# A fused attention, expert and gated-product kernel: unit stores moved earlier, three low-part subtractions per expert change given to GpSimd, and the first gather reordered

## The chip, the cores and the metric

The kernel runs on one core of a Trainium2 chip. The metric is device time in microseconds (us) of one execution. The engines are called as the profile calls them: PE (TensorE, the matmuls), DVE (VectorE), ACT (ScalarE), POOL (GpSimd) and SP (SyncE, which here only issues DMAs).

## What is computed

Three parts follow each other, on 4 x 448 = 1792 tokens of 768 numbers:

```python
scores = q @ k.T / sqrt(64) - log(448)
x = sigmoid(scores) @ v                       # 4 batches, 12 heads of 64
e = argmax(cosine(x, expert_emb) / tau)       # one of 8 experts for each token
y = gate_w * (relu(x @ w1[e]) @ w2[e])        # w1 768x1024, w2 1024x768
out = ((y @ w_a) * (y @ w_b)) @ w_out         # 768x1536, 768x1536, 1536x768
```

## The kernel before, in words

**Arithmetic in two parts.** A product in float32 is made of three cheaper ones: every operand is split into a high part, rounded by a copy, and a low part, the operand minus the high part. `split` (line 786) does it for weights: ACT copies the raw tile to the high part (line 787), and an engine, `nc.vector` unless told otherwise, subtracts (line 788). PE multiplies high by high, high by low and low by high.

**Attention** (`attention`, line 492) is a loop over 24 pairs of heads, numbers 0 to 23, with one more turn to drain. A turn transposes q and k of the next pair (`tr_pair`, line 554), loads q, k and v of later pairs (`load`), computes scores and sigmoids in two halves (matmul line 579, ACT line 584), multiplies by v (line 601), and turns the outcome to tokens (`x_tok`, lines 616 and 617). Between these steps `pump` advances generators that hold the routing of a finished batch (`route`) and the tables of a half of the tokens (`tables`): which tokens stand in which block of 128, and which expert a block has. Once the flags of the first half stand, `first_expert` returns seven small steps, an empty one and six that split one slice of `w1` of the first expert each and load the slice after the next (lines 917 to 931). One is taken per turn from `early_w`, and what is left runs after the loop. When the tables stand, `gather(0)` (line 812, an indirect DMA issued by POOL) fetches the tokens of the first block.

**Background units.** The weights of the third part are rounded ahead of time in 144 units, of which 48 run in the first two parts. `prep_tick` (line 231) does four things for successive units: it stores finished ones (`prep_store`, line 226, a DMA on SP's queue), finishes one (`prep_finish`, DVE line 216, two operands in SBUF), loads one (`prep_load`, SP) and begins one (`prep_unit`: DVE lines 199 and 201, ACT lines 203 and 205, POOL line 206). The tile `ab`, which ACT writes at line 205, has three buffers, so a unit waits until the store of the unit three before has read its own. In attention most turns have one tick at their end, the turns 9, 15 and 21 two.

**Experts.** `block1` (line 990) handles one block of 128 tokens: first matmul `p1` (line 891, or 911 to 913 for the first block), turning of the hidden layer and its split (ACT 969 and 970, DVE 973, tile `hTl`), and second matmul `p2` (line 1012). All weights of an expert lie in SBUF as high and low parts, `w1h`/`w1l` in six slices of 1024 columns and `w2h`/`w2l` in eight of 768. Where the next block has another expert, the flag `chg` is 1 and its 14 slices are split inside the block and the next one, in this order on ACT and DVE: `w1` slices 0 and 1, the tokens of the next block (`x_load`, DVE line 841), `w1` slices 2 to 5, a tick, the block's output `y` (DVE 1082), `prep_finish`, `w2` slices 0 to 3; in the next block `w2` slices 4 and 5 after its first `p1` and 6 and 7 in its second. The raw weights of the expert after that are loaded by SP in the block that uses the earlier ones: `load_new(1)` at its beginning, `load_new(2)` after its first tick, each into tiles that the splits must have left. POOL has, in order, the gather for the block after the next, the additions of the ticks and the scatter of `y` (line 1104). Each engine works its queue in program order.

**The third part** (`glu`) streams the rounded weights and is not touched.

The change moves three lines of `attention`, a `prep_store()` of `block1`, and adds an engine argument in `split_w` (line 801).

Of the kernel before, what the change touches and what calls it, by code (L numbers as in the profile page):

```python
# [9 lines left out]
F32 = mybir.dt.float32  # L10
# [14 lines left out]
def build(ctx: ExitStack, tc: tile.TileContext, q, k, v, emb, tau, w1, w2, wa, wb, wo, out, dbg=None, stop=None):  # L25
# [6 lines left out]
    nc = tc.nc  # L32
# [193 lines left out]
    def prep_store(dma=nc.sync):  # L226
        while prep_out:
            o, t = prep_out.pop(0)
            dma.dma_start(out=o, in_=t)
# [248 lines left out]
    def pump(ps=(True, LATE, END)):  # L478

        while bg:  # L480
            job = next((j for j in bg if j[2]), bg[0])
            if job[1] and job[1] not in ps:
                return
            job[2] = False
            try:
                job[1] = next(job[0])
                return
            except StopIteration:
                bg.remove(job)


    def attention():
# [21 lines left out]
        def load(i, names):  # L514
            if i >= NPR:
                return
            b, hp = pairs[i]
            for nm in names:
                src = dict(q=q, k=k, v=v)[nm]
                sv = src[b, 2 * hp:2 * hp + 2].rearrange("h (p c) d -> p h c d", c=NCH)  # L520
                if nm == "v":
                    t = raw_p.tile([P, 2, NCH, D], F32, tag=nm, name=nm, bufs=4)
                    nc.sync.dma_start(out=t[:, :, :NCH - 1, :], in_=src[b, 2 * hp:2 * hp + 2, :KC].rearrange(
                        "h (p c) d -> p h (c d)", c=NCH - 1))
                    nc.sync.dma_start(out=t[half_of(i), :, NCH - 1, :],
                                      in_=src[b, 2 * hp:2 * hp + 2, KC:].rearrange("h p d -> p h d"))
                elif nm == "k":
                    t = raw_p.tile([P, NCH, 2, D], F32, tag=nm, name=nm, bufs=3)
                    dma = nc.scalar if i < 2 else nc.sync
                    for j in range(2):  # L530
                        dma.dma_start(out=t[:, :NCH - 1, j, :], in_=src[b, 2 * hp + j, :KC].rearrange(
                            "(p c) d -> p c d", c=NCH - 1))
                    nc.sync.dma_start(out=t[half_of(i), NCH - 1], in_=src[b, 2 * hp:2 * hp + 2, KC:].rearrange(
                        "h p d -> p h d"))
                else:
                    t = raw_p.tile([CP, NCH, 2, D], F32, tag=nm, name=nm, bufs=3)
                    for j in range(2):
                        nc.sync.dma_start(out=t[:, :, j, :], in_=sv[:, j])
                raw[i, nm] = t

        def tr_pair(i):

            if i == 1:
                pt = [p() for p in av_ps]
                parts = [(pt[s][:, :S], slice(s, s + 1)) for s in range(2)]
            else:
                both = ps_t.tile([P, 2, 512], F32, tag="pt", name="pt")
                pt = [both[:, s] for s in range(2)]
                parts = [(both[:, :, :S], slice(0, 2))]
            for s, nm in enumerate(("q", "k")):  # L550
                t = raw.pop((i, nm))
                for c in range(NCH):
                    cs, r = (slice(c * CP, (c + 1) * CP), slice(0, CP)) if nm == "q" else key_chunk(i, c)
                    nc.tensor.transpose(out=pt[s][:, cs], in_=t[r, c].rearrange("p h d -> p (h d)"), identity=ident[r, r])
            hi = qk_p.tile([P, 2, S], F32R, tag="qkh", name="qkh")
            lo = qk_p.tile([P, 2, S], F32R, tag="qkl", name="qkl")
            for src, ss in parts:
                h, l = (t[:, ss, :] if src.ndim == 3 else t[:, ss.start, :] for t in (hi, lo))
                nc.scalar.copy(out=h, in_=src)
                nc.vector.tensor_tensor(out=l, in0=src, in1=h.bitcast(F32), op=ALU.subtract)  # L560
            QK[i] = (hi, lo)
# [83 lines left out]
        for i in range(NPR + 1):  # L645
            if 0 < i and i + 1 < NPR:
                tr_pair(i + 1)
            load(i + 3, "qk")
            load(i + 2, "v")
            if i < NPR:  # L650
                score_half(i, 0)
            misc["ps"] = av_ps[i % 2]
            if i == NPR:
                one, turn = misc["ps"], [0]

                def either():
                    turn[0] ^= 1
                    return ps_s.tile([P, 2, 512], F32, tag="ps", name="pm2")[:, 0] if turn[0] else one()

                misc["ps"] = either  # L660
            pump((True,))
            if early_w is None and misc.get("flags0"):
                early_w = first_expert()
            if misc.get("tables0") and not misc.get("gathered"):
                gather(0)
                misc["gathered"] = True
            if early_w:
                early_w.pop(0)()
            if 1 <= i <= NPR:
                av_part(i - 1, 0)  # L670
            pump((True,))
            if i < NPR:
                score_half(i, 1)
            pump((LATE,))
            if i % 2 and i >= 2:
                x_tok(i - 2)
            if 1 <= i <= NPR:
                av_part(i - 1, 1)
            if i == NPR:
                both = ps_s.tile([P, 2, 512], F32, tag="ps", name="px0")  # L680
                x_load(0, [both[:, hf] for hf in range(2)])
                gather(1)
            if i >= 2:
                if i % 2 == 0:
                    x_tok(i - 2)
                b, hp = pairs[i - 2]
                if hp == NP - 1:
                    routed(b)
            if i < 3:
                prep_load(i)  # L690
            elif i < NPR:
                prep_tick(nc.sync)
                if i % 6 == 3 and i > 3:
                    prep_tick(nc.sync, 1)
            pump((END,))

        while early_w:
            early_w.pop(0)()
# [87 lines left out]
    def split(hi, lo, src, f32_hi, eng=nc.vector):  # L786
        nc.scalar.copy(out=hi, in_=src)  # L787
        eng.tensor_tensor(out=lo, in0=src, in1=f32_hi, op=ALU.subtract)  # L788
# [8 lines left out]
    def load_w(which, expert, pair):  # L797
        t, src = (r1[pair], w1) if which == 1 else (r2[0][:, 2 * pair:2 * pair + 2, :], w2)
        nc.sync.dma_start(out=t, in_=src[expert, 2 * pair * P:2 * (pair + 1) * P, :].rearrange("(k p) c -> p k c", p=P))

    def split_w(which, kk, pool=None):
        hi, lo = (w1h, w1l) if which == 1 else (w2_t["h"], w2_t["l"])
        t = r1[kk // 2][:, kk % 2, :] if which == 1 else r2[0][:, kk, :]
        split(hi[kk], lo[kk], t, hi[kk].bitcast(F32))

    def gather(b):
        if b >= NBLK:
            return
        ph = 0 if b < LIVE0 else 1
        t = xg_t[b % len(xg_t)]  # L810
        j = b - TB[ph][0]
        nc.gpsimd.indirect_dma_start(out=t, out_offset=None, in_=xs_d[:CAP[0], :] if ph == 0 else xs_d[:, :],
                                     in_offset=bass.IndirectOffsetOnAxis(ap=idx[ph][:, j:j + 1], axis=0))
        xg[b] = t
# [166 lines left out]
    def moe(r2_p):  # L981
# [8 lines left out]
        def block1(b, chg, was_new, load, e_load, live):  # L990
            def when_new(fn, chg=chg):
                if chg is not None:
                    with tc.If(chg == 1):  # L993
                        fn()

            def load_new(which):
                for i in range((KD if which == 1 else KF) // 2):
                    load_w(which, e_load, i)
# [5 lines left out]
            def p1(hf, inner):  # L1004
                p1_half(b, hf, ps_1.tile([P, FH], F32, tag="p1", name="p1"),
                        mx_p.tile([P, FH], F32, tag="h", name="h"), inner)
# [31 lines left out]

            if b > 0:
                when_new(lambda: load_new(1), load)  # L1040
                p1(0, lambda: None)
                when_new(lambda: split_new(2, KF // 2, KF - 2), was_new)
                tick()

                def rest():
                    when_new(lambda: split_new(2, KF - 2, KF), was_new)

                p1(1, rest)
                tick()
                if b < LIVE - 1:  # L1050
                    prep_tick()
                when_new(lambda: load_new(2), load)
# [37 lines left out]
                    nc.vector.scalar_tensor_tensor(out=yo[:PH], in0=yp[hf][PH:, :HD], scalar=gt[:PH], in1=yo[:PH],  # L1090
                                                   op0=ALU.mult, op1=ALU.add)

            if 0 < b < LIVE - 1:
                prep_store()
            either(b, y_whole, y_half)
            if live is not None:
                tc.mark_branch_hint_location(f"live{b + 1}", live, [ET.Activation, ET.DVE])
# [8 lines left out]

        for i in range(2, KF // 2):
            load_w(2, e_of[0], i)

        def block(b, was_new=None):  # L1110
            nx = b + 1
# [253 lines left out]
```

## Time and profile before

| what | us |
|---|---|
| median of 3 runs (lowest, highest) | 1075.32 (1074.67, 1077.29) |
| the profiled execution, its own time | 1076.83 |
| its span, first to last instruction | 1074.9 |

In the profiled execution the first turns of attention begin near 14 us, attention ends near 210 us, the blocks of tokens run to about 538 us, and the third part to the end. The profile says for each engine how long it was busy, which instruction ended each idle stretch, and what clock was granted to PE. An instruction that had to wait after it was begun shows a longer time, not an idle stretch. A row of the timeline merges equal instructions that follow each other (x4), and its time runs from the first's start to the last's end.

### The profile page before, as it was taken

The page shows a single profiled execution, that of the slowest core. Times are in us where ns is not written, and L with a number is a line of the kernel's source. Part 1 is how long each engine was busy: PE and PEld are TensorE (multiplying, and loading weights), DVE is VectorE, ACT ScalarE, POOL GpSimd, SP SyncE. Part 2 cuts the span into 40 slices and gives each one's busy share as a digit, 9 for nine tenths or more (in the row PEclk, how much of TensorE's full clock was granted, in tenths as well). Part 3 has the DMA queues.
Part 4 walks back from the last instruction along what each step waited for, and adds up shares of the span by engine and source line. Part 5 has one row for each costly group of instructions (what it writes and reads, how often), then busy time and mean ns, then how long its engine had stood idle before and what let it go on. Part 6 is the DMA issues. An engine that isn't in the chain of part 4 may idle for free. (4 is left out here: it accounts for less than half of the span.)

```text
span 1074.9 us, 17443 instructions
## 1 busy us (share of the span) xinstructions
PE 1049.5 (98%) x5916; PEld 848.5 (79%) x5916; DVE 592.3 (55%) x1061; ACT 510.4 (47%) x803; POOL 154.2 (14%) x222
## 2 busy tenths in 40 slices
PE   7999999999999999999999999999999999999998
PEld 4554555488878977998978888888888888888997
DVE  2566698868793869372256786333333333333553
ACT  5777676543673777262155554333323322332542
POOL 2031221423222222221102222000000000000000
PEclk9999999999999999999999999999999999999999
DMA  6687769648589778822184644292220272210820
GB/s 161 170 207 200 186 175 260 197 146 292 174 307 331 253 262 305 317 86 101 47 279 176 221 132 145 105 361 109 88 88 1 107 289 89 89 45 1 350 105 30
DMA packets 118051, 187.84 MB, mean 175 GB/s; under 512 B 53928, under 2 KB 89000, under 8 KB 113072
## 3 DMA queue, kind: packets, MB, share of 16 engines
q1 hardware_dynamic: 113296, 171.10, 47.5%
q0 software_dynamic: 3040, 14.94, 3.9%
q8 instruction: 56, 0.92, 0.3%
q10 hardware_dynamic: 1600, 0.39, 0.2%
q14 instruction: 59, 0.48, 0.1%
HBM read 154.17 MB, written 32.24 MB: 173 GB/s over the span
## 5 line engine op out<-in xcount | busy, mean ns | idle before, releaser
L1229 PE MATMUL ab<-yh,whi 128*128 128x512 f32 (+1 forms) x576 | 209.3, 363 | 0.4 <-DVE yl L788 0.4
L1230 PE MATMUL ab<-yl,whi 128*128 128x512 f32 (+1 forms) x576 | 209.3, 363 | 0.2 <-DVE yl L788 0.2
L1231 PE MATMUL ab<-yh,wlo 128*128 128x512 f32 (+1 forms) x576 | 209.0, 363 | 0.0
L206 POOL TENSOR_TENSOR m<-m,raw 128x384 int32<-128x384 int32 x72 | 75.9, 1054 | 353.8 <-DVE m L201 193.4
L1231 PEld LDWEIGHTS ab<-yh,wlo 128*128 128x128 f32 x576 | 108.8, 189 | 17.3 <-DVE wlo L788 0.3
L1229 PEld LDWEIGHTS ab<-yh,whi 128*128 128x128 f32 x576 | 108.8, 189 | 16.3 <-ACT whi L787 0.5
L1230 PEld LDWEIGHTS ab<-yl,whi 128*128 128x128 f32 x576 | 108.8, 189 | 16.2 <-DVE yl L788 0.9
L1262 PE MATMUL o<-whi,gh 128*128 128x512 f32 x336 | 114.7, 341 | 0.0
L1263 PE MATMUL o<-whi,gl 128*128 128x512 f32 x336 | 113.7, 338 | 0.0
L1264 PE MATMUL o<-wlo,gh 128*128 128x512 f32 x336 | 113.0, 336 | 0.0
L1237 DVE TENSOR_TENSOR m<-ab,a 128x512 f32<-128x512 f32 (+1 forms) x48 | 30.0, 624 | 144.6 <-issue 126.5
L787 ACT CAST gh<-m 128x512 fp32r<-128x512 f32 (+1 forms) x48 | 27.2, 567 | 166.4 <-DVE m L1237 166.4
L584 ACT ACTIVATE a<-ps,bias_s 128x896 f32<-128x896 f32 x96 | 92.9, 1006 | 26.5 <-PE ps L579 25.8
L788 DVE TENSOR_TENSOR wlo<-r,whi 128x768 fp32r<-128x768 f32 x76 | 68.6, 954 | 57.3 <-ACT whi L787 57.3
L787 ACT CAST whi<-r 128x768 fp32r<-128x768 f32 x76 | 58.9, 833 | 54.6 <-PE o L1263 46.0
L601 PE MATMUL av<-a,v 128*64 128x448 f32 (+1 forms) x384 | 79.8, 571 | 2.0 <-DVE xtok L617 2.0
L788 DVE TENSOR_TENSOR wlo<-wx,whi 128x768 fp32r<-128x768 f32 x57 | 51.2, 954 | 44.0 <-ACT whi L787 44.0
L1262 PEld LDWEIGHTS o<-whi,gh 128*128 128x128 f32 x336 | 63.4, 189 | 8.2
L1263 PEld LDWEIGHTS o<-whi,gl 128*128 128x128 f32 x336 | 63.4, 189 | 7.5
L1264 PEld LDWEIGHTS o<-wlo,gh 128*128 128x128 f32 x336 | 63.1, 188 | 7.4
L973 DVE SCALAR_TENSOR_TENSOR hTl<-px,hTh 128x512 fp32r<-128x512 f32 x35 | 24.1, 689 | 73.2 <-ACTq L993 63.7
L787 ACT CAST whi<-wx 128x768 fp32r<-128x768 f32 x57 | 43.8, 832 | 40.7 <-PE o L1263 36.0
(271 smaller groups left out, 1847.6 us busy)
## 6 DMA issues: line engine op xcount, KB each, us to landing
r<-in_moe_w_dram SPq DMA_DIRECT2D x28, 768.0 KB, 14.6
wx<-wm SPq DMA_DIRECT2D x18, 1152.0 KB
r<-wm SPq DMA_DIRECT2D x17, 1152.0 KB, 5.6
r<-in_moe_w_dram SPq DMA_DIRECT2D x18, 1024.0 KB, 10.9
raw<-in_moe_w_a_dram SPq DMA_DIRECT2D x24, 384.0 KB, 3.7
raw<-in_moe_w_b_dram SPq DMA_DIRECT2D x24, 384.0 KB, 3.7
raw<-in_moe_w_out_dram SPq DMA_DIRECT2D x24, 384.0 KB, 3.9
wm<-ab SPq DMA_DIRECT2D x48, 192.0 KB, 2.6
```

The lines of the kernel that those rows point to most:

```text
L206: nc.gpsimd.tensor_tensor(out=m, in0=m, in1=low, op=ALU.add)
L584: nc.scalar.activation(out=a[r], in_=ps[:n, :, :S], func=AF.Sigmoid, bias=bias_s[:n], scale=qscale)
L601: nc.tensor.matmul(av[w][j * D:(j + 1) * D, :S], lhsT=raw[w, "v"][r, j, c, :], rhs=a[r, j, :], start=first, stop=last)
L787: nc.scalar.copy(out=hi, in_=src)
L788: eng.tensor_tensor(out=lo, in0=src, in1=f32_hi, op=ALU.subtract)
L1229: nc.tensor.matmul(ps[:, :n], lhsT=hi[:, s, cs], rhs=yh[:, kk, :n], start=kk == 0, stop=False)
L1230: nc.tensor.matmul(ps[:, :n], lhsT=hi[:, s, cs], rhs=yl[:, kk, :n], start=False, stop=False)
L1231: nc.tensor.matmul(ps[:, :n], lhsT=lo[:, s, cs], rhs=yh[:, kk, :n], start=False, stop=kk == KD - 1)
L1237: nc.vector.tensor_tensor(out=m, in0=ps[:, :n], in1=a, op=ALU.mult)
L1262: nc.tensor.matmul(t[:, d0:d1], lhsT=gh[:, cs], rhs=hi[:, 2, d0:d1], start=first, stop=False)
L1263: nc.tensor.matmul(t[:, d0:d1], lhsT=gl[:, cs], rhs=hi[:, 2, d0:d1], start=False, stop=False)
L1264: nc.tensor.matmul(t[:, d0:d1], lhsT=gh[:, cs], rhs=lo[:, 2, d0:d1], start=False, stop=last)
```

## The change

In attention, finished units are stored at the beginning of a turn, ahead of its loads; the step of `early_w` is taken before the turn's first `pump`, where it was taken after it (so the first, empty one is taken a turn later); and `gather(0)` goes out at the end of the turn in which the tables are done, where it went out in the next turn after the first `pump`. In `block1` the store of finished units goes from the end of the block to the beginning of the next, behind `load_new(1)`. From the first block on, GpSimd does the subtraction of slice 3 of `w1` and of slices 2 and 5 of `w2`.

```diff
@@ attention, in a turn
             if 0 < i and i + 1 < NPR:
                 tr_pair(i + 1)
+            prep_store()
             load(i + 3, "qk")
             load(i + 2, "v")
...
+            if early_w:
+                early_w.pop(0)()
             pump((True,))
             if early_w is None and misc.get("flags0"):
                 early_w = first_expert()
-            if misc.get("tables0") and not misc.get("gathered"):
-                gather(0)
-                misc["gathered"] = True
-            if early_w:
-                early_w.pop(0)()
...
             pump((END,))
+            if misc.get("tables0") and not misc.get("gathered"):
+                gather(0)
+                misc["gathered"] = True
@@ split_w
+    on_pool = {}
+
     def split_w(which, kk, pool=None):
...
-        split(hi[kk], lo[kk], t, hi[kk].bitcast(F32))
+        split(hi[kk], lo[kk], t, hi[kk].bitcast(F32), nc.gpsimd if kk in on_pool.get(which, ()) else nc.vector)
@@ block1
             if b > 0:
                 when_new(lambda: load_new(1), load)
+                if b < LIVE:
+                    prep_store()
                 p1(0, lambda: None)
...
-            if 0 < b < LIVE - 1:
-                prep_store()
             either(b, y_whole, y_half)
@@ moe, before block(0)
+        on_pool.update({1: (3,), 2: (2, 5)})
```

## Rows read from the trace of the kernel before

**Rows 1.** The page, busy time of each engine (share of the span) and instructions.

```profile
PE 1049.5 (98%) x5916; PEld 848.5 (79%) x5916; DVE 592.3 (55%) x1061; ACT 510.4 (47%) x803; POOL 154.2 (14%) x222
```

**Rows 2.** Waits of PE, whole run: us in total, times, longest.

```profile
PE ps L579 <- ACT a L584: 1.6, 1, 1.6
...
PE p L1012 <- ACT hTh L970: 1.5, 2, 0.7
...
PE px L962 <- ACT h L914: 1.3, 3, 0.8
```

**Rows 3.** Stretches: length, busy us of the engines, granted clock, DMA share, GB/s.

```profile
106.00:109.00 3.00, 3.00 (x13) 1.28 (x10) 0.62 (x1) 2.35 (x4) 0.00 (x0) 0.50 0.68 195
...
284.00:305.00 21.00, 21.00 (x115) 19.00 (x114) 20.68 (x28) 17.82 (x28) 5.71 (x5) 1.00 0.69 248
...
460.00:480.00 20.00, 19.96 (x111) 18.04 (x110) 17.19 (x20) 15.56 (x24) 5.01 (x2) 1.00 0.14 46
```

**Rows 4.** Timeline of attention, turns 10 to 12, DVE, SP and ACT: start, us, what.

```profile
92.48 1.02 DVE L216 SCALAR_TENSOR_TENSOR ab<-ab,m 128x384 f32<-128x384 f32 x2
...
99.59 1.01 SPq L229 DMA_DIRECT2D wm<-ab  x2
...
102.19 0.56 ACT L205 ACTIVATE ab<-raw 128x384 f32<-128x384 bf16 x1 [3.91 <-DMA wm<-ab]
```

**Rows 5.** Timeline behind the end of attention: DVE and PE.

```profile
212.90 0.69 DVE L617 COPY xtok<-pm 112x512 f32<-112x512 f32 x1
...
214.64 0.39 PE L912 MATMUL p<-w1l,xh 128*128 128x512 f32 x1
```

**Rows 6.** Timeline, POOL and DVE at three places.

```profile
300.55 1.02 POOL L206 TENSOR_TENSOR m<-m,raw 128x384 int32<-128x384 int32 x1 [6.91 <-DVE m L201]
...
300.82 2.97 DVE L788 TENSOR_TENSOR w1l<-r,w1h 128x1024 fp32r<-128x1024 f32 x2
...
303.71 1.01 DVE L841 TENSOR_TENSOR xl<-px,xh 128x384 fp32r<-128x384 f32 x2
...
388.08 2.36 DVE L788 TENSOR_TENSOR w1l<-r,w1h 128x1024 fp32r<-128x1024 f32 x2 [0.25 <-ACT w1h L787]
...
205.35 2.06 POOL L206 TENSOR_TENSOR m<-m,raw 128x384 int32<-128x384 int32 x1 [5.65 <-ACT w1h L787]
...
206.46 0.98 DVE L311 TENSOR_SCALAR om<-sg 112x32 f32<-112x32 f32 x1
```

**Rows 7.** Groups of POOL instructions by shape: busy us, mean ns.

```profile
L377 POOL TENSOR_TENSOR py<-oh_all,beg 112x64 f32<-112x64 f32 x2 | 0.6, 322 | 0.2
```

**Rows 8.** Timeline at the sixth change of expert: DVE and POOL.

```profile
471.85 5.36 DVE L788 TENSOR_TENSOR w2l<-r,w2h 128x768 fp32r<-128x768 f32 x6
...
472.70 3.56 POOL L1104 DMA_INDIRECT ys<-y,idy  x1 [6.46 <-ACT w2h L787]
```

**Rows 9.** Timeline, second, third and fifth change: DVE makes hTl, PE first uses it.

```profile
318.04 0.68 DVE L973 SCALAR_TENSOR_TENSOR hTl<-px,hTh 128x512 fp32r<-128x512 f32 x1
...
319.95 1.55 PE L1012 MATMUL p<-w2h,hTl 128*128 128x384 f32 x8
...
368.93 0.68 DVE L973 SCALAR_TENSOR_TENSOR hTl<-px,hTh 128x512 fp32r<-128x512 f32 x1
...
370.49 1.55 PE L1012 MATMUL p<-w2h,hTl 128*128 128x384 f32 x8
...
424.90 0.68 DVE L973 SCALAR_TENSOR_TENSOR hTl<-px,hTh 128x512 fp32r<-128x512 f32 x1
...
426.48 1.55 PE L1012 MATMUL p<-w2h,hTl 128*128 128x384 f32 x8
```

**Rows 10.** Timeline between the first and the second change: SP and ACT.

```profile
289.20 0.34 SPq L229 DMA_DIRECT2D wm<-ab  x1
...
291.28 1.74 SPq L799 DMA_DIRECT2D r<-in_moe_w_dram  x3
...
304.50 2.00 ACT L787 CAST w1h<-r 128x1024 fp32r<-128x1024 f32 x2 [1.63 <-DMA r<-in_moe_w_dram]
```

## The prediction, made before the changed kernel was run

> **What bounds the kernel now.** I read the busy times first: PE is busy 98% of the span [rows 1], so the other engines matter only where PE waits for them, or where a change makes it wait. Next came the waits of PE. They are few, and three kinds matter here: one wait of 1.6 us in attention for ACT's sigmoids, and 1.5 and 1.3 us (five waits in all) in the expert part for ACT's copies of the hidden layer [rows 2]. Then the stretches: around the first two changes of expert, which follow in successive blocks, DVE is busy 20.68 of 21 us while PE loses nothing [rows 3]. The fourth and fifth change also follow each other and repeat that. So PE sets the time, and DVE is full exactly where the change puts its hand. There are six changes of expert in the run: two such pairs, a lone third one and a lone sixth one, which has no background units.
>
> The sum is made against the profiled execution, 1076.83 us by its own time. That is 1.5 us above the median of 1075.32, and I move the sum to the median at the end.
>
> **Earlier stores in attention.** In turn 11 ACT stood 3.91 us before it could write `ab`, until a store of `ab` had landed [rows 4]. DVE had finished that tile and its neighbour by 93.5 (92.48 and 1.02), but SP issued the two stores only at 99.59, behind the loads of turn 11 [rows 4]. A store at the beginning of the turn goes out near 93.5. With the time from issue to landing that this one took (102.19 less 99.59, 2.6 us) it lands near 96.1, while ACT needs the tile at 98.3 (102.19 less 3.91). So ACT's wait goes, and with it PE's wait of 1.6 us for the sigmoids [rows 2]. Behind that wait PE ran at a granted clock of 0.50, the 1.2 GHz level, from 106 to 109 us [rows 3]; three us at half speed cost 1.5 more. **Gain: 3.1 us.** Ends: 0, if something else holds ACT there, and 3.1. The loads that now stand behind the two stores are 1.0 us later (the two issues took 1.01 [rows 4]), and they serve a turn two or more later; if that cover went, it would be 1.0 us once. PE waited for the sigmoids this once only [rows 2], so no second such wait comes forward.
>
> **The steps of the first expert.** Each moves later by a little under a turn, so the sixth, taken inside the last turn before, now runs behind the loop: one copy on ACT and one low part on DVE. In DVE's queue it stands just before the copy that began at 212.90, so it ends near 214.1 (1.18 us, below), and PE first reads it at 214.64 [rows 5]. Cost: nothing, with 0.5 us of cover; ends minus 1.2 and plus 1.2, its own length taken off or put on PE's path. **The gather** keeps its place on POOL's queue: both the old and the new place lie behind the two unit additions of turn 21 and ahead of the routing of the third batch, since the pump between them gives POOL nothing. Cost: nothing, both ends.
>
> **Three low parts on POOL.** What DVE saves: six subtractions of 768 columns took 5.36 us [rows 8], 0.89 each, and two of 1024 columns 2.36 [rows 6], 1.18 each, so 2 x 0.89 + 1.18 = 2.96 us per change. What POOL needs: its addition of 384 columns took 1.02 us [rows 6], its product of 64 columns 0.322 [rows 7], so 0.70 us for 320 columns; along that line 768 columns take 1.86 and 1024 take 2.42 us, 6.14 per change.
>
> Whether they run beside each other decides. The rows say no: while POOL added at 300.55 to 301.57, DVE's two subtractions from 300.82 on took 2.97 us instead of 2.36 [rows 6]; they began to move when POOL was done. The other way round, POOL's addition at 205.35 took 2.06 instead of 1.02 behind a subtraction of DVE; and when it then ran, DVE's next instruction, a tiny one, took 0.98 us [rows 6], so a waiting POOL came in between two instructions of DVE. If that holds, each moved subtraction stops DVE for POOL's time: 6.14 - 2.96 = 3.18 us more per change in a full stretch. The end on the good side is that DVE keeps its 2.96 and is never stopped. DVE instructions with one operand in PSUM may run beside POOL: two of `xl` (1.01 us, [rows 6]) and one `hTl` (0.68, [rows 9]) stand in the chain, so up to 1.7 us per change may be hidden. I take 1.0, a little over half, since slice 3 is ready about when `xl` is due and slice 5 only sometimes near `hTl`. That leaves **2.2 us per change**.
>
> The Trainium skill, SBUF — State Buffer, Who interferes with whom, says that a DVE instruction with two SBUF inputs and a GpSimd instruction that reads SBUF exclude each other for the whole instruction, and that one with at most one SBUF input is free of this. It speaks against the change: by it no subtraction overlaps another. The traces agree on the first half by the 2.97 us above; with nothing hidden its sum is that of the fourth case below.
>
> What of it PE sees is read at `hTl`, the last tile that DVE makes behind the `w2` slices: at the second change DVE is done 1.23 us before PE needs it (318.72, 319.95), at the fifth 0.90 (425.58, 426.48), at the third 0.88 (369.61, 370.49) [rows 9]. DVE is full through each pair, so both changes add up there: 4.4 - 1.23 = 3.2 us and 4.4 - 0.90 = 3.5. The third gives 2.2 - 0.88 = 1.3. The sixth gives nothing: DVE has idle time there (17.19 of 20 busy [rows 3]). **Loss: 8.0 us.** Ends: minus 2.8 (next part) and 6.36 + 6.36 + 3.18 - 3.01 = 12.9.
>
> The Trainium skill, GPSIMD Engine Reference, Performance versus the Vector engine, has 4497 ns for an addition of 2048 columns; an estimate from it is 1.69 and 2.25 us for ours, 2.67 instead of 3.18 us more per change, and the loss would be 5.3 instead of 8.0 us. The rows of this run stand in the sum.
>
> **The store at the block's end.** SP issued the store of a finished unit at 289.20, when DVE had come to it, and so the three loads of `w1` for the second change only at 291.28; ACT later waited 1.63 us for one of them [rows 10]. With the store behind `load_new(1)`, two of the three loads go as soon as their tiles are free, some us earlier. The waits of PE on ACT, 1.5 + 1.3 = 2.8 us [rows 2], lie in these pairs and would go. But `hTl` is then late through DVE, so PE waits there instead: gain 0 beside the loss above, 2.8 without it.
>
> **Sum:** 1076.83 - 3.1 + 8.0 = 1081.7 for the profiled execution, 1080.2 against the median.
>
> **Rivals.**
> *DVE keeps the port (faster).* At the sixth change POOL's scatter took 3.56 us beside a chain of six subtractions that itself ran at 5.36 [rows 8]: POOL waited, DVE did not. If POOL waits for the end of a chain, the chain of four ends 1.8 us earlier, `hTl` follows, and slices 2 and 5 come beside it. Then DVE has its 2.96 us, and the waits of 2.8 and the 3.1 of attention go: 1075.3 - 5.9 = 1069.4. Against it stands the 0.98 us row of rows 6. It decides if POOL starts a subtraction only where DVE's chain pauses. Chance 0.32.
> *The two cancel (the same).* POOL stops DVE, but what is hidden is 1.7 us per change, so 1.5 are left: 3.0 - 1.2 + 3.0 - 0.9 + 1.5 - 0.9 = 4.5 loss, less 3.1 and about 1 of the loads' gain, 1075.7. Chance 0.20.
> *Nothing is hidden (slower still).* 12.9 - 3.1 = 9.8, 1085.1; a long wait may also drop PE's clock, as at 106 to 109 us. Chance 0.18.
> The forecast itself has 0.30.
>
> **How the numbers follow.** A difference under 0.3%, 3.2 us, can't be told from none here. Faster is the first rival, 0.32; the same is the second, 0.20; slower is the forecast and the last rival, 0.48. Faster and slower both hold much, so the range goes over both: from 1068 (the first rival and 1.2 of the steps) to 1088 (all of the 12.9 without the gain in attention). The forecast's own range is 1077 to 1085.
>
> **What would show it.** In attention ACT's wait before `ab` in turn 11 and the 0.50 clock behind it are gone. POOL shows subtractions of 1.9 and 2.4 us or longer, DVE subtractions beside them stretched by as much, and the waits of PE name DVE at `hTl` or `w1l` at five of the six changes, 2 to 4 us in each pair. If DVE's chains keep 0.89 and 1.18 us per subtraction while POOL's are stretched, the first rival is right and the forecast wrong in sign. If the wait in turn 11 stays, the store was not what held ACT.

## The result, and the profile after

The changed kernel takes 1088.68 us (median of 5 runs, 1087.39 to 1091.12) against 1075.32: ratio 1.0126, 95% interval 1.0111 to 1.0141. It is slower, as forecast, but by 13.4 us and not by 4.9, and 0.7 us beyond the upper end of the range. The profiled execution took 1087.39 us with a span of 1085.7; 10.8 us more than the span of before, 1074.9.

The page's busy times, which answer to [rows 1]:

```profile
PE 1051.1 (97%) x5916; PEld 850.9 (78%) x5916; DVE 606.2 (56%) x1042; ACT 510.1 (47%) x803; POOL 188.9 (17%) x241
```

DVE has 19 instructions fewer and is busy 13.9 us longer: work was taken from it, and it has become slower. The waits of PE, changed kernel (us in total, times, longest; [rows 2]):

```profile
PE p L1015 <- DVE w2l L789: 8.0, 7, 1.7
...
PE p L894 <- DVE xl L844: 4.7, 2, 2.4
PE p L1015 <- DVEq L996: 3.5, 5, 1.8
```

The waits for ACT's `a`, `hTh` and `h` have left the list; in their place PE waits for three tiles of DVE. PE runs the same 5916 matmuls in the same order in both kernels, so the start of the same matmul in both traces says how far PE is behind, and the difference between two places says where it lost:

| matmul at | before | after | behind by |
|---|---|---|---|
| end of turn 12 of attention | 109.29 | 105.92 | -3.4 |
| end of attention | 209.00 | 205.08 | -3.9 |
| second block of tokens (block 1), `hTl` | 242.77 | 242.23 | -0.5 |
| before the first change of expert | 262.71 | 262.62 | -0.1 |
| end of the first pair of changes | 318.06 | 321.59 | +3.5 |
| end of the third change | 368.09 | 373.74 | +5.7 |
| end of the second pair | 424.59 | 435.09 | +10.5 |
| end of the experts | 538.13 | 548.83 | +10.7 |

Attention gives 3.9 us. The experts take back 14.6 us: 3.4 in block 1, 0.4 more up to the first change, 3.6 and 4.9 in the pairs, 2.1 at the third change, 0.2 behind it (from the starts to a hundredth; the table is rounded). The last column is a balance: in the pairs PE also got rid of waits, of which more below.

Where PE stood, from the timeline of PE, changed kernel (block 1, first change, start of the next block, second change):

```profile
237.42 0.62 PE L1015 MATMUL p<-w2h,hTl 128*128 128x384 f32 x2 [1.78 <-DVEq L996]
...
297.79 0.62 PE L1015 MATMUL p<-w2l,hTh 128*128 128x384 f32 x2 [1.74 <-DVE w2l L789]
...
308.88 1.67 PE L894 MATMUL p<-w1h,xh 128*128 128x512 f32 x6 [2.35 <-DVE xl L844]
...
321.13 0.62 PE L1015 MATMUL p<-w2l,hTh 128*128 128x384 f32 x2 [1.73 <-DVE w2l L789]
```

And why, from the timelines of DVE and of POOL, changed kernel, first change and the one behind it ([rows 6] show two of the same places before):

```profile
291.98 2.18 DVE L216 SCALAR_TENSOR_TENSOR ab<-ab,m 128x384 f32<-128x384 f32 x1 [0.24 <-POOL m L206]
294.08 5.39 DVE L789 TENSOR_TENSOR w2l<-r,w2h 128x768 fp32r<-128x768 f32 x4
...
303.19 5.17 DVE L789 TENSOR_TENSOR w1l<-r,w1h 128x1024 fp32r<-128x1024 f32 x2
308.28 1.01 DVE L844 TENSOR_TENSOR xl<-px,xh 128x384 fp32r<-128x384 f32 x2
...
284.54 2.59 POOL L789 TENSOR_TENSOR w1l<-r,w1h 128x1024 fp32r<-128x1024 f32 x1 [4.41 <-ACT w1h L788]
...
291.90 1.84 POOL L789 TENSOR_TENSOR w2l<-r,w2h 128x768 fp32r<-128x768 f32 x1
...
295.05 1.85 POOL L789 TENSOR_TENSOR w2l<-r,w2h 128x768 fp32r<-128x768 f32 x1
302.90 1.03 POOL L206 TENSOR_TENSOR m<-m,raw 128x384 int32<-128x384 int32 x1 [6.00 <-ACT xh L834]
304.87 2.40 POOL L789 TENSOR_TENSOR w1l<-r,w1h 128x1024 fp32r<-128x1024 f32 x1 [0.93 <-ACT w1h L788]
307.43 1.79 POOL L815 DMA_INDIRECT xg<-xs,idx  x1
```

POOL's slice 2 of `w2` (291.90 to 293.74) ran straight behind its addition, and DVE's line 216, begun at 291.98, took 2.18 instead of 0.56 us. Slice 5 (295.05 to 296.90) came between DVE's slices 0 and 1 of `w2`: four subtractions took 5.39 where six took 5.30 with nothing on POOL. Slice 1 is what PE waits for at 297.79. At the second change POOL's addition and its slice 3 of `w1` came before and between DVE's slices 0 and 1 of `w1`: two subtractions took 5.17, where [rows 6] have 2.97. The tokens' low part `xl` stands behind them, and PE, at the start of the next block, waits 2.35 us for it.

In attention the store went out as written, though it landed later. Timelines of DVE, SP and ACT, changed kernel, against [rows 4]:

```profile
92.58 1.02 DVE L216 SCALAR_TENSOR_TENSOR ab<-ab,m 128x384 f32<-128x384 f32 x2
...
93.67 2.29 SPq L229 DMA_DIRECT2D wm<-ab  x2
...
99.01 0.56 ACT L205 ACTIVATE ab<-raw 128x384 f32<-128x384 bf16 x1 [0.64 <-DMA wm<-ab]
```

The stores go out 5.9 us earlier, ACT waits 0.64 instead of 3.91 us, and PE does not wait for the sigmoids. From issue to landing the store now took 5.3 us (99.01 less 93.67), where the prediction took over 2.6; that is why 0.64 us of ACT's wait is left. Stretches, changed kernel (columns as in [rows 3]):

```profile
105.00:108.00 3.00, 3.00 (x26) 2.25 (x24) 2.61 (x7) 2.84 (x5) 0.00 (x0) 1.00 0.84 195
...
236.00:243.00 7.00, 5.58 (x27) 5.55 (x28) 4.11 (x13) 0.94 (x3) 1.12 (x2) 0.76 0.28 96
284.00:309.00 25.00, 20.91 (x112) 18.26 (x111) 24.11 (x23) 20.94 (x33) 15.23 (x9) 1.00 0.93 328
422.00:427.00 5.00, 4.67 (x13) 3.72 (x14) 4.97 (x8) 2.52 (x4) 0.66 (x1) 0.66 0.34 102
```

The granted clock of 0.50 in turn 12 is gone, and lower clocks stand in two new places, behind the wait in block 1 (0.76) and behind the second wait for `xl` (0.66). In the pair (284 to 309) DVE does 23 instructions in 24.11 us; before it did 28 in 20.68 [rows 3].

### The profile page after: what moved, and what is told of

Read it like the earlier page. It is cut to its first block, busy times and chain, and to the rows that moved or that the text cites. A ratio compares the mean times of both kernels' runs of the same rounds, so it can differ in the third digit from the quotient of the medians.

```text
span 1085.7 us, 17566 instructions
## 1 busy us (share of the span) xinstructions
PE 1051.1 (97%) x5916; PEld 850.9 (78%) x5916; DVE 606.2 (56%) x1042; ACT 510.1 (47%) x803; POOL 188.9 (17%) x241
## 4 chain that ended last, share of the span: by engine, by line
PE 52%; DVE 1%; issue 0%; ACT 0%; POOL 0%; ACTq 0%; POOLq 0%
PE ab L1235 11%; PE ab L1234 11%; PE ab L1236 11%; PE o L1267 6%; PE o L1268 5%; PE o L1269 5%; PE p L1015 2%; PE p L894 2%; PE ab L784 0%; DVE yl L789 0%; PE px L965 0%; PE px L784 0%; DVE wlo L789 0%; PE px L963 0%; DVE y L1087 0%
## 5 line engine op out<-in xcount | busy, mean ns | idle before, releaser
L1015 PE MATMUL p<-w2h,hTl 128*128 128x384 f32 x288 | 60.2, 344 | 3.5 <-DVEq L996 3.5
```

What stands on the lines that cost most here:

```text
L1015: nc.tensor.matmul(yp[hf][:, :HD], lhsT=l[:, kk, :], rhs=wv[kk][:, hf * HD:(hf + 1) * HD], start=kk == 0 and i == 0 and len(parts) == 2, s ...
```

## The experiments

"None on POOL" below is the kernel of the first experiment. Each ratio is to runs of the kernel before on the same chip. A difference between two experiments is the difference of their ratios, times 1075.3 us.

**The parts, each alone.** Four kernels: the changed one without its table of slices, and the kernel before with one part each.

```diff
no_pool (from the changed kernel)
-        on_pool.update({1: (3,), 2: (2, 5)})
pool_only (from the kernel before)
+        on_pool.update({1: (3,), 2: (2, 5)})
att_only (from the kernel before): the hunk in attention
moe_store_only (from the kernel before): the two hunks of prep_store in block1
```

> The changed kernel with all fourteen low parts on DVE again; the stores, the first gather and the loads stay moved. Theory A (the three subtractions on POOL are the whole loss of 14.6 us in the expert part, the moved stores only gain): 3.9 us less than before in attention, and the waits of PE on ACT for the weights and the hidden layer, 2.8 us, gone at the pairs of changes, so 1075.3 - 6.7 = about 1068.6, between 1067 and 1071. Theory B (a part of the loss comes from the moved store or from the earlier loads, which meet other DMAs, or DVE is too full at the pairs with its own 14 slices to use them): 1071.4 (attention alone) or more; above 1075 if the moved stores cost what POOL is blamed for.

> The kernel before with the three subtractions per change on POOL and nothing else. Theory A (all of the loss is POOL's): the changed kernel less its gains, 1088.7 + 3.9 + 2.8 = about 1095, at least 1090. Since the late loads can hide behind the waits for DVE, the 2.8 may not come on top: then 1092.6. Theory B (the loss needs the moved stores too): 1084 or less. At the first turned block, where PE waited 1.78 us for the low part of the hidden layer, the wait should be near nothing if the 3.9 us that PE gained in attention made it, and the same if POOL's own slice did.

> The kernel before with the three moved lines of attention alone. Theory A: the wait of ACT in turn 11 and the stretch at the lower clock behind it are gone as in the changed kernel, 1075.3 - 3.9 = 1071.4. Theory B (PE's lead of 3.9 us is eaten at the first turned block, where DVE comes behind the routing): 1073 to 1075, with a new wait of PE of 1 to 2 us near 235 us.

> The kernel before with the store of finished units behind the loads of the first weights in the expert part alone. Theory A: the two pairs of changes lose their waits of PE on ACT (2.8 us): 1072.5, with the second change's loads of the first weights issued some 8 us earlier. Theory B (the earlier loads help nothing while DVE subtracts all fourteen slices, since DVE is the next to be late): within 1 us of 1075.3, with PE waiting for DVE's low parts at the pairs instead.

| kernel | median us | ratio to before (95%) |
|---|---|---|
| no_pool | 1071.98 | 0.9966 (0.9954 to 0.9978) |
| pool_only | 1091.68 | 1.0140 (1.0125 to 1.0156) |
| att_only | 1073.13 | 0.9975 (0.9966 to 0.9984) |
| moe_store_only | 1075.38 | 0.9993 (0.9984 to 1.0002) |

POOL's three slices are the whole loss: alone they cost 15 us, and without them the rest of the change is 3.7 us faster than before. **None on POOL is faster than the kernel before and than the changed one**; att_only lies within its interval. Its gain is smaller than the 6.7 us that I expected. Attention gives 2.7 us and not 3.9. A likely reason, not shown: the profiled execution of before had lost 1.5 us to the lower clock behind its wait (moe_store_only too: 0.50 from 106 to 109 us); pool_only, which keeps that wait, did not (waits of PE and stretches, pool_only):

```profile
PE ps L579 <- ACT a L584: 1.5, 1, 1.5
```

```profile
104.00:106.00 2.00, 1.76 (x14) 0.95 (x16) 0.37 (x1) 1.87 (x3) 0.00 (x0) 1.00 1.04 177
106.00:109.00 3.00, 3.00 (x25) 2.12 (x26) 2.11 (x5) 2.62 (x5) 0.00 (x0) 1.00 0.80 225
```

The moved store in the expert part gives 0.8 us alone, with an interval that holds zero, and not 2.8: Theory B. SP does issue the three loads of `w1` 7.4 us earlier (against 291.28 in [rows 10]; timeline of SP, moe_store_only):

```profile
283.88 5.77 SPq L799 DMA_DIRECT2D r<-in_moe_w_dram  x3
```

and PE then waits for DVE (waits of PE, moe_store_only):

```profile
PE p L891 <- DVE w1l L788: 1.3, 2, 0.6
...
PE p L1012 <- DVE hTl L973: 0.9, 2, 0.5
```

The trace of moe_store_only shows more than the runs do: between the end of attention and the end of the experts PE gains 2.0 us on the kernel before. Just behind, some of it is given back: from 540 to 542 us the granted clock was 0.50 there and 1.00 before. So whether the moved store is worth 0.8 or 2.0 us stays open.

In pool_only PE also falls 1.7 us further behind at block 1's `hTl`, without any lead from attention; in no_pool it has the lead and loses only 0.1 there. So POOL's own slice made that wait, not the lead.

**Is it the exclusion, or the order?** POOL does the same amount again behind DVE's own subtraction, into the raw tile that is done with; once by subtracting, once by filling with zeros.

```diff
 dup_sub, split_w, from no_pool
-        split(hi[kk], lo[kk], t, hi[kk].bitcast(F32), nc.gpsimd if kk in on_pool.get(which, ()) else nc.vector)
+        split(hi[kk], lo[kk], t, hi[kk].bitcast(F32))
+        if kk in on_pool.get(which, ()):
+            nc.gpsimd.tensor_tensor(out=t, in0=t, in1=hi[kk].bitcast(F32), op=ALU.subtract)
 block1, from no_pool
                 split_new(2, 4, KF)
+                on_pool.update({1: (3,), 2: (2, 5)})
 dup_fill, from dup_sub
-            nc.gpsimd.tensor_tensor(out=t, in0=t, in1=hi[kk].bitcast(F32), op=ALU.subtract)
+            nc.gpsimd.memset(t, 0.0)
```

> The version with nothing on POOL (1072.0), and POOL does in addition, behind DVE's own, the subtractions of slice 3 of w1 and 2 and 5 of w2 again, into the raw tile that is done with. DVE saves nothing, so only the exclusion is left: 2 x 1.86 + 2.42 = 6.14 us per change at five full changes. Theory A (POOL reading SBUF and DVE's subtractions shut each other out): 15 to 30 us more, 1087 to 1102, DVE's chains longer by POOL's times. Theory B (what cost time was the order of the tiles, DVE being late only where POOL delivers late): nobody waits for POOL's outcome but the reload of the raw tiles, 1072 to 1076.

> The same, but POOL fills those raw tiles with zeros where it subtracted: it writes SBUF and reads none. If it is POOL's reading that shuts DVE out: 1072 to 1074, and DVE's chains of six subtractions keep 5.3 us beside the fills. If any work of POOL on SBUF does it: longer by the fills' own time at five changes (with fills of 1 to 2 us each, 1080 to 1095).

dup_sub: 1099.20 us, ratio 1.0190 (1.0173 to 1.0207), 24 us more than none on POOL. dup_fill: 1072.78 us, ratio 0.9967 (0.9946 to 0.9988), the same as none on POOL. Timelines of DVE and POOL at the first change's `w2`, dup_sub:

```profile
294.32 6.95 DVE L789 TENSOR_TENSOR w2l<-r,w2h 128x768 fp32r<-128x768 f32 x6
...
297.09 2.49 POOL L809 TENSOR_TENSOR r<-r,w2h 128x768 f32<-128x768 f32 x1 [3.28 <-DVE w2l L789]
```

and the same place in dup_fill:

```profile
288.65 5.30 DVE L789 TENSOR_TENSOR w2l<-r,w2h 128x768 fp32r<-128x768 f32 x6
...
291.39 0.74 POOL L809 MEMSET r<- 128x768 f32 x1 [3.26 <-DVE w2l L789]
```

No engine waits for what POOL makes here except the reload of the raw tile, and still the subtraction costs 24 us and the fill nothing. The reload is not what costs: PE's waits for ACT's `w1h`, which follows it, are 0.9 us in all in both runs. Nor are the conditions that POOL now evaluates, since dup_fill has them too. DVE's chain of six is 1.65 us longer beside a subtraction that takes 1.85 when nothing holds it, and keeps its 5.30 beside a fill. The fills are shorter (0.74 and 0.96 us), but by the rival they would have cost 2.4 us a change. So it is POOL's reading. The Trainium skill, SBUF — State Buffer, Who interferes with whom, names just this pair, two SBUF inputs on DVE against a GpSimd instruction that reads SBUF and not one that only writes; both halves are borne out by these runs.

Two things in dup_sub go beyond that (timelines of DVE and POOL, second change). First, POOL did not come in between two subtractions here: DVE's chain of six kept 5.30 us, and POOL's 1.85 us of work took 4.23, until DVE had come to `hTl`, which has one operand in PSUM and kept its 0.68 us beside POOL. Slice 2 of `w2` did the same at the sixth change; at the other four it came in. Second, line 199 of DVE, which has only one input in SBUF, took 2.19 instead of 0.35 us beside a subtraction of POOL (and 1.18 to 1.19 us beside POOL's additions, seven times in the third part of the kernel before). So the prediction's sentence that an instruction with at most one SBUF input is free of this holds here for `hTl` and not for line 199. The section of the Trainium skill that it cites excepts the two-port modes of DVE, which the sentence left out; whether line 199 ran in one, no run shows.

```profile
320.38 5.30 DVE L789 TENSOR_TENSOR w2l<-r,w2h 128x768 fp32r<-128x768 f32 x6
325.59 0.68 DVE L978 SCALAR_TENSOR_TENSOR hTl<-px,hTh 128x512 fp32r<-128x512 f32 x1
...
328.98 2.19 DVE L199 TENSOR_SCALAR m<-raw 128x384 int32<-128x384 int32 x1
...
323.14 4.23 POOL L809 TENSOR_TENSOR r<-r,w2h 128x768 f32<-128x768 f32 x1 [3.74 <-DVE w2l L789]
...
329.09 1.86 POOL L809 TENSOR_TENSOR r<-r,w2h 128x768 f32<-128x768 f32 x1
```

**One slice at a time.** In these five kernels POOL's table is filled behind the first block's split of `w2`, so that slice stays on DVE.

```diff
 block1, from no_pool
                 split_new(2, 4, KF)
+                on_pool.update(table)
table: block0_dve {1: (3,), 2: (2, 5)}; only_w1 {1: (3,)}; only_w2a {2: (2,)}; only_w2b {2: (5,)}; w1_slice5 {1: (5,)}
```

> The changed kernel, but the first block's slice 5 of w2 stays on DVE; POOL subtracts from the second block on. Theory A (POOL's 1.88 us there hold back the gather and the fourteen small steps of the routing behind it on POOL, and so the output of the first block and the low part of the hidden layer): the wait of 1.78 us near 237 us and the low clock behind it, 3.4 us together, are gone: 1088.7 - 3.4 = 1085.3. Theory B (PE's lead of 3.9 us out of attention makes that wait, since DVE's own branch there takes 1.95 us either way): the wait stays, 1088 to 1089. The kernel without any subtraction on POOL already speaks for A.

> As the run with the first block's slice on DVE, but POOL subtracts slice 3 of w1 alone. It shuts DVE out for 2.4 us per change where DVE saved 1.18. Against the version with none on POOL (1072.0): Theory A (a slack that all three slices draw on): at the second change of a pair DVE is 2 to 3 us later at the tokens' low part, PE waits about 1 us there twice, 2 to 4 us in all: 1074 to 1076. Theory B (each slice costs its own exclusion at the place where it stands, whatever the others do): the two waits of 2.4 us for the tokens' low part stay whole: 1077 or more.

> POOL subtracts slice 2 of w2 alone (first block on DVE). Theory A (shared slack): slice 2 shuts DVE out 1.84 us ahead of w2's first slices, the slack of 1.4 to 2.6 us at the second of them covers it nearly: 1072 to 1075. Theory B (each costs its own): of the four waits of 1.9 to 2.0 us at that slice about half stays: 1076 or more.

> POOL subtracts slice 5 of w2 alone (first block on DVE). Theory A (shared slack): 1.85 us of exclusion, in among w2's first slices, covered by the slack of 1.4 to 2.6 us at the second: 1072 to 1075. Theory B (each costs its own): 1076 or more. If slices 2 and 5 of w2 and 3 of w1 come to much less together than 1085 - 1072 = 13 us when each is alone, the slack was shared; if their three losses add up to 13, it was not.

> POOL subtracts slice 5 of w1 instead of slice 3, and nothing of w2 (first block on DVE). With slice 3 it was 1078, and the loss of 5.4 us was two waits of 2.4 us for the tokens' low part. Theory A (the place decides: slice 3 is ready on ACT while DVE still has slice 1 and the tokens in front of it, slice 5 only later): the waits for the tokens' low part are gone, 1073 to 1075.5. Theory B (the sum decides: DVE is full through the pair, 2.4 - 1.18 = 1.2 us per change are lost wherever they stand): about 1077 to 1078, with the waits at the low part of the hidden layer or at w1 instead.

The fourth column is how much further PE fell behind none on POOL between the end of attention and the end of the experts, from the starts of the same matmuls as in the table of the result.

| kernel | ratio to before (95%) | over none on POOL, us | by the traces, us |
|---|---|---|---|
| only_w1 | 1.0016 (1.0005 to 1.0028) | 5.4 | 5.3 |
| only_w2a | 0.9999 (0.9988 to 1.0009) | 3.5 | 2.5 |
| only_w2b | 0.9998 (0.9988 to 1.0008) | 3.4 | 3.9 |
| block0_dve | 1.0119 (1.0078 to 1.0160) | 16.5 | 12.7 |
| w1_slice5 | 1.0002 (0.9993 to 1.0012) | 3.9 | 4.2 |

Each costs by itself, and the three together (12.7 by the traces) cost little more than their sum (11.7). There is no slack that covers one and not three: Theory B. By their ratios only_w2a and only_w2b, at 1075.2 and 1075.1 us, lie between the ranges of the two theories; it is the sum that decides. A granted clock of 0.50 behind waits for `xl` makes 1.4 us of only_w1's figure (413 to 416 us) and 3.1 of block0_dve's (307 to 310 and 420 to 423); without it the sum is 10.3 against 9.6, and the finding is the same. What does change is the place. Waits of PE, only_w1:

```profile
PE p L894 <- DVE xl L844: 4.8, 2, 2.4
```

and only_w2b:

```profile
PE p L1015 <- DVE hTl L976: 3.1, 4, 1.0
```

and w1_slice5:

```profile
PE p L894 <- DVE w1l L789: 2.9, 6, 0.6
```

Slice 3 of `w1` alone makes both waits for `xl` whole. The waits of 1.7 us at slice 1 of `w2` need both slices of `w2`; with one of them PE waits mainly at `hTl` instead (3.1 us above, 2.4 in only_w2a, where 0.5 are left at `w2l`; 1.5 with none on POOL). With slice 5 of `w1` the waits for `xl` are gone, as Theory A said, but nearly the whole loss is met at `w1l`, as Theory B said. Whether slice 5 is a little cheaper than slice 3 (3.9 against 5.4 us) the intervals leave open; in the traces the difference is the lower clock in only_w1.

block0_dve's four runs lie between 1084.05 and 1092.97 us, too wide to show the 3.4 us by time. Its trace shows them. Block 0 in the changed kernel, timelines of POOL, DVE:

```profile
222.68 1.88 POOL L789 TENSOR_TENSOR w2l<-r,w2h 128x768 fp32r<-128x768 f32 x1 [15.55 <-PE p L1015]
225.42 1.67 POOL L815 DMA_INDIRECT xg<-xs,idx  x1 [0.86 <-POOLq L996]
...
236.68 0.69 DVE L976 SCALAR_TENSOR_TENSOR hTl<-px,hTh 128x512 fp32r<-128x512 f32 x1 [1.95 <-DVEq L996]
```

and in block0_dve:

```profile
223.57 0.95 POOL L815 DMA_INDIRECT xg<-xs,idx  x1 [16.77 <-PE px L784]
...
234.86 0.69 DVE L976 SCALAR_TENSOR_TENSOR hTl<-px,hTh 128x512 fp32r<-128x512 f32 x1 [1.95 <-DVEq L996]
```

With the slice on DVE the gather issues 1.85 us earlier, and with it the fourteen small steps of the last batch's routing that stand behind it on POOL, the routing's steps on DVE that wait for them, block 0's output and block 1's `hTl` behind that in DVE's queue (1.82 us earlier). PE's wait of 1.78 us in block 1 is gone: Theory A. A part comes back in the next block: before the first change of expert PE waits there for `hTl` 1.44 us, against 1.07 in the changed kernel. So the net price of the slice is a little under 3 us.

**The store alone in attention.** One run of the kernel before with only the first `prep_store()` added.

> The kernel before with the earlier store in attention alone, the first expert's steps and the gather where they were. Theory A: 3.3 us of the 3.9 in attention are the store's; the last 0.5 to 0.6 (a wait of PE for the slots of the first half, near 166 us, gone) are from the steps taken before the first pump, and stay away here: 1072 to 1074 for the one run. Theory B: all of it is the store's, and the same 0.5 us are gained.

1074.25 us for the one run. PE is 3.3 us ahead at the end of turn 12, all of it the store's. The wait of 0.4 us for the first half's slots near 166 us (line 458) is gone here too. But the granted clock was 0.76 from 162 to 167 us (1.00 in att_only), which took over 1 us back, most of it ahead of that wait; so whether the wait went because PE came later, or would have gone without the earlier step anyway, this run does not show. What the reordered steps are worth by themselves stays open.

## Why the prediction was right and wrong

**Right.** *PE sets the time, DVE is full at the pairs.* The new waits of PE in the result all name DVE. *Earlier stores in attention:* 3.1 us forecast, 3.4 in the profile; of it the 1.5 for the clock is not lost in every execution, which may be why the runs gave 2.7 for all of attention. *First expert's steps and gather:* no cost; no wait appeared there. *POOL's times:* 1.86 and 2.42 forecast, 1.85 and, unhindered, 2.40 measured. *They exclude each other, and a waiting POOL comes in between two instructions of DVE:* shown by dup_sub and dup_fill, and by the rows of the changed kernel above; only twice in dup_sub did POOL wait past two more subtractions. With that the first rival (DVE keeps the port, 0.32) falls as the account of this kernel: for a subtraction of POOL its mechanism is seen in those two places alone. The second (the two cancel) falls as well.

**Wrong: "What of it PE sees is read at `hTl`".** This is the step that failed, three times over. *First,* the credit of 1.0 us per change for running beside `xl` and `hTl` was not there. Such an instruction can run beside POOL (`hTl` in dup_sub above), but here none stood in the right place. What POOL takes, it takes when its input is ready, and ACT, which makes that input, runs ahead of DVE; so slice 3 ran behind `xl` at the first change and before it at the second, each time in among DVE's slices of `w1`, slice 2 right behind POOL's addition and slice 5 between DVE's first two slices of `w2`. *Second,* the slack of 1.23 and 0.90 us at the end of the chain is no allowance for the chain's middle: PE waited at `w2l` slice 1 and at `xl`, which are needed earlier, and each change of a pair paid there. *Third,* the slices before the first change were costed at nothing because I looked at changes of expert only; block 0's slice 5 of `w2` is split outside any change, and there POOL was the head of a chain (gather, routing, output, `hTl`). It cost 3.4 us in block 1: 1.86 as the wait and 1.5 as the lower clock behind it.

The term was 8.0 us. At the places it was summed over (3.2, 1.3 and 3.5) the balance was 3.6, 2.1 and 4.9, 10.6 together, 1.4 of that the lower clock behind a wait; outside them 4.0 were lost.

**Wrong: the loads' gain.** I put 0 beside the loss and 2.8 without it. Beside the loss, PE's waits on ACT did shrink: from 2.2 us in the first pair and 1.9 in the second to 0 and 0.9. But in pool_only, where no store is moved, they shrink to the same 0 and 0.9: a PE that comes late finds ACT ready. Without the loss the moved store gave 0.8 us by the runs and 2.0 by the trace of the experts; the waits for DVE that came up (`hTl` 0.9, `w1l` 0.7 more) are part of what is missing.

**The rivals.** Nothing hidden (1085.1, chance 0.18) had the mechanism and named the clock; what it left out is block 0. The exclusion's net price of 3.18 us per change, times the five full changes, is 15.9; the traces have 12.7 for it. The forecast's 8.0 took 7.9 off: 3.0 as slack, with rows but at the wrong tile, and 5 for running beside `xl` and `hTl`, with no row that showed POOL's work falling there.

## What to carry to other kernels

A subtraction of two SBUF tiles moved from a full DVE to POOL costs up to POOL's time less DVE's, here 0.5 to 1.1 us a slice at each of five changes (2.5 to 5.3 us in all by the traces), because neither reads beside the other; POOL's free time is not DVE's to use, unless POOL only writes. When an engine becomes later, look for the first tile behind the delay that its reader needs soon, not for the slack at the end of the chain, and also go through the places where the same helper is called outside the loop that one has in mind. Run a bundle of edits part by part: here 3.7 us of gain were hidden in a change that lost 13.4.

## What the hardware showed that I had not expected

- POOL's fill of 768 columns took 0.74 us and left DVE's chain at 5.30 us; POOL's subtraction of the same tile lengthened it to 6.95.
- A waiting POOL came in between two subtractions of DVE nearly everywhere, but twice in dup_sub it stood through two more of them (4.23 us for 1.85 us of work).
- A wait of PE of the same length need not bring the lower clock: 1.6 us in attention were followed by a granted clock of 0.50 before ([rows 3]), 1.5 us at the same place by 1.00 in pool_only.
- In block 1, DVE stood 1.95 us in its own sequencer between the output of block 0 and `hTl`, in the changed kernel and in block0_dve alike (1.96 before). It is a fixed link of the chain by which POOL's delay reached PE.
